# FFT long convolution and token mixer on one core: the first two second-stage chunks of the next group issued inside the inverse's first stage

## The chip, the cores and the metric

The kernel runs on one core of a Trainium2 chip. The metric is the device time of one execution in microseconds (us): 2053.82 us is the median of three runs (2049.52 to 2056.14).

The engines are named as the profile names them. PE is the matrix engine (TensorE) and PEld its weight loads, DVE is VectorE, ACT is ScalarE, POOL is GpSimd, and SP issues DMA transfers. PE can write only into PSUM, so each result has to be copied out by ACT or DVE; such a copy is called an eviction here.

## The reference

The first half is a long convolution along the sequence, done by FFT; the second is a token mixer.

```python
x, h: (8, 5696, 128), (5696, 128)
Xf = rfft(x, n=2 * S, axis=1); Hf = rfft(h, n=2 * S, axis=0)
x = irfft(Xf * Hf, n=2 * S, axis=1)[:, :S, :]
theta = x @ w_theta
zr, zi = x * cos(theta), x * sin(theta)
y = einsum('ts,bsd->btd', w_tok_r, zr) + einsum('ts,bsd->btd', w_tok_i, zi)
u = x + y
out = u + relu(u @ w_ch)          # w_tok_r, w_tok_i: (5696, 5696)
```

The change lies in the convolution alone, which fills less than the first fifth of the time. The mixer, whose two weight matrices are streamed in and transposed on the way, takes the rest.

## The kernel before, in words

**Groups.** The 8 batch rows and 128 channels are cut into 8 groups: two batch rows and 64 channels each. A transform of length 11392 is split as 178 x 64, and everything is done with matmuls against tables of sines and cosines. Each group goes through four stages:

- **A** (`stage_a`, matmuls L250): first stage of the forward transform, 16 chunks of 4 matmuls. The result is evicted by ACT (L259) into the tile `a`.
- **F** (`f2`, matmuls L270): second stage of the forward transform, 12 chunks F0 to F11. F0 to F10 have 32 matmuls each, F11 has 8, followed by 12 filler matmuls (L276). Each chunk is evicted by ACT into a tile `xs` (L426, called X here), of which there are two. DVE multiplies `xs` by the spectrum of the filter, `hs`, into `uv_t` (L428, and L433 for the last short chunk): this is the product P.
- **C** (`stage_c`, matmuls L448 and L449): first stage of the inverse, 16 chunks C0 to C15 of 16 matmuls. It reads `uv_t`. Each chunk is evicted into a column block of the tile `g`, by ACT (L453) or by DVE (L455).
- **D** (`stage_d`, matmuls L484): second stage of the inverse, 7 chunks D0 to D6. Each uses `g` over all its columns as weights, so D0 needs the evictions of all 16 C chunks. It is evicted into `yt`, by DVE (L488) for two chunks and by ACT (L490) for the others.

**The order.** The main loop (L772 to L798) has two halves per group g. In the first half, C of group g is mixed with A of group g + 1; I call it the CA half. In the second, D of group g is mixed with F, X and P of group g + 1; I call it the FD half. `woven` (L280) does the mixing: every list of steps gets a stretch of the interval 0 to 1, and the steps are issued in order of their positions. A goes to 0 to 0.88, C to 0.06 to 1.0, so that the tail of C has nothing beside it. There are seven passages from a CA half to an FD half in which both have work of the next group (g = 0 to 6); the eighth group has no successor.

Each engine runs its own instructions in the order of its queue. In the loop's steady state PE's order around the passage is A14 A15 C13 C14 C15 F0 F1 D0 F2 F3 D1 F4 D2 F5 F6 D3 F7 F8 D4 F9 F10 D5 F11 D6, and after it A0 A1 C0 of the next group's CA half.

**Who evicts.** In the CA half ACT takes all of A and the C chunks with `q % 32 == 16`, which are C2, C6, C10 and C14; DVE takes the 12 others. In the FD half ACT takes X0 to X11 and D1, D2, D4, D5 and D6; DVE takes P0 to P11, D0 and D3.

**Buffers.** All four stages draw their PSUM tiles from one pool of four (`fp`, L102), two banks each. There are two `xs` tiles (`fs`, L118) and four `hs` tiles (`fh`, L114). The product of chunk c issues the load of `hs` for chunk c + 4 on SP (L436). The loads of `x` for the group after next are issued by POOL (L153), each behind a small copy that reads an evicted column of `g` (L151).

Of the kernel before, what the change touches and what calls it, by code (L numbers as in the profile page):

```python
# [12 lines left out]
F16 = mybir.dt.float16  # L13
add = mybir.AluOpType.add
mult = mybir.AluOpType.mult
AF = mybir.ActivationFunctionType
# [6 lines left out]
def kernel(  # L23
# [10 lines left out]
    nc = tc.nc  # L34
    B, S, D = x.shape
    assert D == 128
    P = 128
# [42 lines left out]
    CK = 8  # L80
    HD = D // 2
# [5 lines left out]
    CHK = [(c0, min(CK, K1 - c0)) for c0 in range(0, K1, CK)]  # L87
    NCK = len(CHK)
    CN = 10
# [17 lines left out]
    LEAD = 4  # L107
# [11 lines left out]
    fs = pool("fft_s", 2, conv, side="right")  # L119
# [142 lines left out]
    def f2(a_st, c, warm=WARM):  # L262

        c0, ck = CHK[c]
        ps = psum()
        for j in range(ck):
            for ri in range(2):
                for e in range(2):
                    rows = slice(64 * e, 64 * e + 64)
                    nc.tensor.matmul(ps[:, e, j * HD:(j + 1) * HD],  # L270
                                     w_t2[rows, c0 + j, N2 * (1 - ri):N2 * (3 - ri)],
                                     a_st["a"][rows, ri * K1 + c0 + j, :],
                                     start=(ri == 0), stop=(ri == 1))
        if c == NCK - 1:
            for n in range(warm):
                nc.tensor.matmul(ps[:, n % 2, ck * HD:ck * HD + 384], w_t2[:, 2, :P],  # L276
                                 w_t2[:, 0:2, :].rearrange("p k n -> p (k n)"), start=True, stop=True)
        return ps[:, :, :ck * HD].rearrange("p e (k d) -> p e d k", k=ck)

    def woven(*lists):  # L280

        lists = [l if isinstance(l, tuple) else (l, 0.0, 1.0) for l in lists]
        steps = [(w0 + (i + 0.5) / len(l) * (w1 - w0), n, f)
                 for n, (l, w0, w1) in enumerate(lists) for i, f in enumerate(l)]
        for _, _, f in sorted(steps, key=lambda s: s[:2]):
            f()
# [37 lines left out]
    ps = psum()  # L324
# [82 lines left out]
    def stage_b(a_st, dh, warm=WARM, first=False):  # L407

        hs_of = {}

        def load(c):
            if c >= NCK:
                return
            hs = hs_of[c] = fh.tile([P, 2, HD * CK], F16, tag="hs", name="hs")
            if first:
                nc.sync.dma_start(hs[:64], hf_hbm[c, dh, :64])
                nc.sync.dma_start(hs[64:], hf_hbm[c, dh, :64, ::-1, :])
            else:
                nc.sync.dma_start(hs, hf_hbm[c, dh])

        def chunk(c):
            c0, ck = CHK[c]
            hv = hs_of[c].rearrange("p r (d k) -> p r d k", k=CK)
            ps = f2(a_st, c, warm)
            xs = fs.tile([P, 2, HD, CK], F16, tag="xs", name="xs")
            nc.scalar.activation(xs[:, :, :, :ck], ps, AF.Copy)  # L426
            if ck == CK:
                nc.vector.tensor_tensor(  # L428
                    uv[:, :, :, c0:c0 + ck],
                    xs.rearrange("p e d k -> p e (d k)").unsqueeze(1).to_broadcast([P, 2, 2, HD * CK]),  # L430
                    hv.rearrange("p r d k -> p r (d k)").unsqueeze(2).to_broadcast([P, 2, 2, HD * CK]), op=mult)
            for r in range(2 if ck < CK else 0):
                nc.vector.tensor_tensor(  # L433
                    uv[:, 2 * r:2 * r + 2, :, c0:c0 + ck], xs[:, :, :, :ck],
                    hv[:, r:r + 1, :, :ck].to_broadcast([P, 2, HD, ck]), op=mult)
            load(c + LEAD)  # L436
        return [lambda c=c: load(c) for c in range(LEAD)], [lambda c=c: chunk(c) for c in range(NCK)]

    def stage_c(st, last):

        def chunk(q):
            if q == 0:
                st["g"] = fg.tile([P, 2 * N2, P], F16, tag="g", name="g_")
            ps = psum()
            for i in range(8):
                o = ps[:, i // 4, (i % 4) * P:(i % 4 + 1) * P]
                at = (q + i) * K1
                nc.tensor.matmul(o, u_t[:, at:at + P], r_u, start=True, stop=False)  # L448
                nc.tensor.matmul(o[:, 2 * NP:], v_t[:, at:at + P], r_v, start=False, stop=True)  # L449
            g_out = st["g"][:K1, :, q:q + 8]  # L450
            g_in = ps[:K1].rearrange("p a (q c) -> p c (a q)", q=4)
            if (last and q % 16 == 0) or (not last and q % 32 == 16):
                nc.scalar.activation(g_out, g_in, AF.Copy)  # L453
            else:
                nc.vector.tensor_copy(g_out, g_in)  # L455
        return [lambda q=q: chunk(q) for q in range(0, 2 * HD, 8)]
# [16 lines left out]
    def stage_d(st, bp, dh, then=None):  # L473
        def chunk(n0, cn):
            if n0 == 0:
                st["yt"] = fy.tile([P, NB, N2], BF16, tag="yt", name="yt")
            g_, yt = st["g"], st["yt"]
            ps = psum()
            nq = 5 if cn == CN else cn
            for j in range(cn):  # L480
                o = ps[:, j // nq, (j % nq) * NB:(j % nq + 1) * NB]
                terms = terms_of(n0 + j)
                for i, (at, e_) in enumerate(terms):
                    nc.tensor.matmul(o, g_[:K1, at, :], e_, start=(i == 0), stop=(i == len(terms) - 1))  # L484
            y_out = yt[:, :, n0:n0 + cn].rearrange("p m (a q) -> p m a q", q=nq)
            y_in = ps[:, :cn // nq, :nq * NB].rearrange("p a (q m) -> p m a q", q=nq)
            if n0 in (0, 3 * CN):
                nc.vector.tensor_copy(y_out, y_in)  # L488
            else:
                nc.scalar.activation(y_out, y_in, AF.Copy)  # L490
            if n0 + cn == N2:
                if then is not None:
                    then(yt)
                for t0, t1 in [(H, S)] if then else YP:
                    for e in range(2):
                        with tc.issue_after(sides["row"]) if then else ExitStack():
                            (nc.gpsimd if then else nc.sync).dma_start(
                                yt_hbm[dh * HD:(dh + 1) * HD, 2 * bp + e, t0:t1],
                                yt[64 * e:64 * e + 64].rearrange("p m n -> p (m n)")[:, t0:t1])
        return [lambda n0=n0, cn=cn: chunk(n0, cn) for n0, cn in CHN]  # L500
# [4 lines left out]
    def front(g, by_dve=(), a_=None, spare=None):  # L505
        if g >= len(groups):
            return [], [], []
        bp, dh = groups[g]
        x16 = x16s[g].rearrange("p b n d -> p (b n) d")
        steps, a_st = stage_a(lambda q: x16[:NB, :, q], by_dve, a_, spare)  # L510
        return (steps, *stage_b(a_st, dh, WARM if g else WARM // 2, g == 0))

    a0, load0, b0 = front(0, (1, 3, 5, 8, 11, 13), a_0, (1, w_t2[:, 2:5].rearrange("p k n -> p (k n)"), 512 - 4 * K1))
# [258 lines left out]
    for g, (bp, dh) in enumerate(groups):  # L772
        st = {}
        last = g + 1 == len(groups)
        a_, load_, b_ = fronts.pop(g + 1) if g + 1 in fronts else front(g + 1)
        if last:
            for _ in range(3):
                steps0.pop(0)()
        now = ([with_load(steps0.pop(0), n < 6) for n in range(9)] if last else [], 0.0, 0.88)
        c_ = stage_c(st, last)  # L780
        if g == 0:
            ec = []
            swap_rows()
            now = ([lambda: ec.append(e_table(1)), lambda: ec.pop()(), lambda: ec.append(e_table(2)), lambda: ec.pop()(),
                    e_minus],
                   -0.1, 0.6)
        woven((c_, 0.06 if a_ else 0.0, 1.0), (a_, 0.0, 0.88), now, load_, (load_x(g + 2, st), 0.1, 1.02))
        if g == 0:
            ordered.close()
        if g + 2 == len(groups):  # L790
            xin.close()
            open_phases()
            load_ya0()
        now = [steps0.pop(0) for _ in range(5)] if last else []
        woven(b_, (stage_d(st, bp, dh, load_ya1 if last else None), 0.08 if b_ else 0.0, 1.1 if b_ else 1.0), now)
        if g + 2 == len(groups):
            load_ya1(st["yt"], True)
            open_ring()  # L798
# [305 lines left out]
    nxt, second, st = None, None, {}  # L1104
    ordered = ExitStack()
    for i, (k, p, tt, j0, s0, nj) in enumerate(stretches):
# [13 lines left out]
        if (p, tt, j0 + s0) == (0, 1, 0):  # L1120
            with tc.issue_after(sides["late"].ins):
# [4 lines left out]
        woven = (tt is not None and end_of_pair and i + 1 < len(stretches)  # L1126
                 and stretches[i + 1][2] is not None)
# [17 lines left out]
        if tt is None:  # L1145
            if p:
                aside(True, False)
            if first_of_pair:
                q = M1 if p else M3
# [20 lines left out]
            if end_of_pair:  # L1170
# [5 lines left out]
                c, c0 = c_last  # L1176
# [161 lines left out]
```

## Time and profile before

| quantity | value |
|---|---|
| median of three runs | 2053.82 us (2049.52 to 2056.14) |
| the profiled execution, its own time | 2052.18 us |
| its span, first to last instruction | 2050.4 us |
| PE busy | 1959.6 us, 96% of the span |
| DVE / ACT / POOL busy | 1538.9 / 639.9 / 965.2 us |
| mean granted clock of PE | 0.987 |
| FD halves of the 2nd to 7th passage start at | 129.8, 167.5, 205.7, 247.4, 285.9, 322.3 us |
| DVE eviction of one C chunk, L455 | 1219 ns |
| ACT eviction of one C chunk, L453 | 1021 ns |
| ACT eviction of one F chunk, L426 | 1023 ns |
| DVE / ACT eviction of one D chunk, L488 / L490 | 1080 / 917 ns |
| product of one chunk on DVE, L428 | 1224 ns |

The table is read like this. The span of the profiled execution is 1.8 us shorter than its own time, since something runs ahead of the first and behind the last instruction. PE is busy for nearly all of the span, so what counts is where PE stands still, and only that. The seven passages lie between 90 and 346 us; behind them only the last group's inverse belongs to the convolution. Their instructions are alike from the second passage on, so one of them, read closely, stands for the others. In the timeline a row of PE gives the start, the length, the line, the tiles, the count, and in brackets the idle time before it with what ended it.

### The profile page before, as it was taken

Reading aid. Unit: us, or ns where it says so; the run is one execution under the profiler, and the core shown is the slowest. Engines: PE = TensorE matmul, PEld = TensorE weight load, DVE = VectorE, ACT = ScalarE, POOL = GpSimd, SP = SyncE. Lnnn points to the kernel's source line nnn. Section 1 sums busy time; section 2 is a strip of 40 time slices with the busy share of each in tenths; the row PEclk is TensorE's granted clock in tenths of the full one; section 3 lists DMA queues with packets and bytes.
Section 4 is the critical chain, followed back from the end, with each engine's and each line's share of the span. In section 5 each row is a group of like instructions: output and inputs, shape, how many; then the busy total and the mean of one; then the engine's idle time right before and its main releaser. Section 6 shows DMA issues by size and latency. Waiting matters only on the chain.

```text
span 2050.4 us, 42565 instructions
## 1 busy us (share of the span) xinstructions
PE 1959.6 (96%) x16205; PEld 1086.2 (53%) x16381; DVE 1538.9 (75%) x2806; ACT 639.9 (31%) x936; POOL 965.2 (47%) x1769
## 2 busy tenths in 40 slices
PE   7799899799999999999999998999999999999998
PEld 5688888654444444444444443444444444444444
DVE  7787777657788888787867667867777686777767
ACT  6788777872232333333300000011111111111111
POOL 8323312384354545454566454453544535354450
PEclk9899999999999999999999999999999999999999
DMA  9999996999899998999999799797887969788793
GB/s 151 187 180 159 146 171 204 238 293 179 163 179 176 170 180 159 179 173 177 170 168 159 119 251 217 107 152 131 150 145 132 155 124 153 131 150 146 131 156 85
DMA packets 510158, 338.21 MB, mean 165 GB/s; under 512 B 184136, under 2 KB 461256, under 8 KB 509864
## 3 DMA queue, kind: packets, MB, share of 16 engines
q0 software_dynamic: 322368, 157.47, 61.0%
q1 hardware_dynamic: 181600, 166.48, 27.8%
q10 hardware_dynamic: 5984, 11.54, 1.6%
q8 instruction: 128, 2.10, 0.4%
q14 instruction: 78, 0.63, 0.1%
HBM read 379.54 MB, written 95.63 MB: 232 GB/s over the span
## 4 chain that ended last, share of the span: by engine, by line
PE 66%; DVE 3%; DMA 2%; issue 1%; POOL 0%; ACT 0%; DVEq 0%; ACTq 0%; SPq 0%
PE m L1275 62%; DMA b<-z_hbm 1%; DVE c L1282 1%; DVE b L831 1%; PE v L977 1%; PE utp L970 1%; PE m L1279 1%; DVE wt L890 1%; PE theta_ps L560 0%; PE tpz L918 0%; PE m L1162 0%; PE m L1196 0%; POOL ring L676 0%; DMA c<-cp_hbm 0%; DMA wl<-in_moe_w_tok_i_dram 0%
## 5 line engine op out<-in xcount | busy, mean ns | idle before, releaser
L676 POOL DMA_DIRECT2D ring<-in_moe_w_tok_i_dram x720 | 387.9, 546 | 657.7 <-DVE wt L890 576.9
L890 DVE STREAM_TRANSPOSE wt<-ring 128x384 f32<-128x384 f32 (+2 forms) x720 | 360.5, 527 | 127.7 <-PE m L1275 77.7
L676 POOL DMA_DIRECT2D ring<-in_moe_w_tok_r_dram x720 | 386.2, 547 | 142.4 <-DVE wt L890 82.4
L1275 PE MATMUL m<-b,wt 128*128 128x512 bf16 x1605 | 386.6, 380 | 3.7 <-DVE wt L890 1.7
L1275 PEld LDWEIGHTS <-wt 128*128 128x128 bf16 x1804 | 176.3, 98 | 219.5 <-DVE wt L890 7.4
L1282 DVE TENSOR_TENSOR c<-c,m 128x512 f32<-128x512 f32 x412 | 266.8, 674 | 0.4 <-PE m L1275 0.4
L972 ACT ACTIVATE ring<-utp 128x512 bf16<-128x512 bf16 x85 | 50.8, 597 | 582.1 <-PE utp L970 582.1
L428 DVE TENSOR_TENSOR uv_t<-xs,hs 128x2048 f16<-128x2048 f16 x88 | 104.4, 1224 | 29.9 <-ACT xs L426 18.2
L448 PE MATMUL ps<-r_u,uv_t 128*128 128x128 f16 x1024 | 116.5, 219 | 4.7 <-ACT cos L588 1.3
L1196 PE MATMUL m<-b,wt 128*128 128x512 bf16 x471 | 110.3, 379 | 7.6 <-DMA b<-z_hbm 4.2
L967 ACT ACTIVATE ub<-c 128x512 bf16<-128x512 f32 x88 | 55.1, 628 | 192.1 <-DVE c L1237 113.5
L449 PE MATMUL ps<-r_v,uv_t 128*128 128x100 f16 x1024 | 114.1, 207 | 0.5
L153 POOL DMA_DIRECT2D x<-in_x_dram x128 | 97.9, 771 | 22.2 <-POOL x L151 14.9
L426 ACT ACTIVATE xs<-ps 128x1024 f16<-128x1024 f32 x96 | 90.8, 972 | 42.4 <-PE ps L270 21.9
L449 PEld LDWEIGHTS <-uv_t 128*128 128x128 f16 x1024 | 99.9, 98 | 7.1 <-issue 5.7
L448 PEld LDWEIGHTS <-uv_t 128*128 128x128 f16 x1024 | 100.0, 98 | 1.1 <-DVE uv_t L433 0.4
L1196 PEld LDWEIGHTS <-wt 128*128 128x128 bf16 x528 | 50.4, 98 | 65.1 <-issue 8.4
L562 ACT ACTIVATE red<-theta_ps,magic 128x512 f32<-128x512 f32 (+1 forms) x46 | 31.6, 687 | 153.1 <-PE theta_ps L560 80.4
L270 PEld LDWEIGHTS <-w_t 64*128 64x128 f16 x3240 | 59.4, 100 | 32.1 <-issue 23.3
L920 ACT ACTIVATE ring<-tpz 128x512 bf16<-128x512 bf16 (+1 forms) x46 | 27.5, 597 | 132.6 <-PE tpz L918 116.3
L250 PE MATMUL ps<-f_t,x 89*128 89x180 f16 x512 | 62.8, 252 | 2.1 <-DVE a L257 1.1
L831 DVE TENSOR_TENSOR b<-b 128x1024 bf16<-128x1024 bf16 x100 | 61.4, 685 | 0.0
(2924 smaller groups left out, 3746.7 us busy)
## 6 DMA issues: line engine op xcount, KB each, us to landing
ring<-in_moe_w_tok_r_dram POOLq DMA_DIRECT2D x352, 96.0 KB, 4.6
ring<-in_moe_w_tok_i_dram POOLq DMA_DIRECT2D x352, 96.0 KB, 4.9
ring<-in_moe_w_tok_r_dram POOLq DMA_DIRECT2D x352, 80.0 KB, 4.5
ring<-in_moe_w_tok_i_dram POOLq DMA_DIRECT2D x352, 80.0 KB, 4.0
cp_hbm<-c SPq DMA_DIRECT2D x88, 256.0 KB, 2.6
c<-cp_hbm SPq DMA_DIRECT2D x88, 256.0 KB, 4.5
out_dram<-c SPq DMA_DIRECT2D x88, 256.0 KB, 4.5
hs<-hf_hbm SPq DMA_DIRECT2D x84, 256.0 KB, 3.4
```

The costliest lines, as they stand in the source:

```text
L153: nc.gpsimd.dma_start(x16[p0:p1, e, n0:n0 + 16, :HD], bass.AP(tensor=src.tensor, offset=src.offset + (p0 * N2 + n0) * D + dh * HD, ap=[[N2 ...
L250: nc.tensor.matmul(ps[:, i // 2, (i % 2) * 2 * K1:(i % 2 + 1) * 2 * K1], lhs(q + i), f1_t[:NB], start=True, stop=True)
L426: nc.scalar.activation(xs[:, :, :, :ck], ps, AF.Copy)
L428: nc.vector.tensor_tensor(uv[:, :, :, c0:c0 + ck], xs.rearrange("p e d k -> p e (d k)").unsqueeze(1).to_broadcast([P, 2, 2, HD * CK]), hv. ...
L448: nc.tensor.matmul(o, u_t[:, at:at + P], r_u, start=True, stop=False)
L449: nc.tensor.matmul(o[:, 2 * NP:], v_t[:, at:at + P], r_v, start=False, stop=True)
L676: nc.gpsimd.dma_start(wb[32 * i:32 * i + 32, :ng, :nj * 64], bass.AP(tensor=a.tensor, offset=a.offset + row0 * S + p * H + i * QR + j0 * 6 ...
L831: return [lambda f=f, x=x: f(*x) for f, x in ((nc.vector.tensor_sub, (bt[M3], b12, b22)), (nc.vector.tensor_sub, (bt[M4], b21, b11)), (nc. ...
L890: nc.vector.transpose(wt.rearrange("p j t r -> p (j t r)").bitcast(F32).rearrange("p (j g t) -> p g j t", j=TJ, g=4)[:, :ng, :nj], wb[:, : ...
L1196: nc.tensor.matmul(ms[n // 2 * 2 + h], a[n][:, j, :, r], bts_of[p][jj][n % 2 * 2 + h][:, r, :], start=(n % 2 == 0 and jj == 0 and r == 0), ...
L1275: nc.tensor.matmul(ms[q], a[q][:, j, :, r], bts[jj][q][:, r, :], start=(jj == 0 and r == 0), stop=(jj == NJ - 1 and r == 1 and q not in left))
L1282: nc.vector.tensor_tensor(c, z, ms[q], op=op)
```

## The change

It has four edits, all in the convolution.

1. `chunk` of the forward second stage is cut into `spectrum` (the matmuls F and the eviction X) and `products` (P and the next load of `hs`). For every group but the first, the spectra of chunks 0 and 1 become the first two steps of the list, and their products the next two.
2. In the main loop the first two steps of that list are taken out of the FD half and woven into the CA half, at 0.84 to 1.0. The products stay behind, at the head of the FD half. A's stretch is shortened from 0.88 to 0.82.
3. Of the C chunks ACT now takes those with `q % 48 == 32`, which are C4 and C10. DVE takes the 14 others, among them C11 to C15.
4. D0 is evicted by ACT, no longer by DVE, except in the last group.

```diff
+        def spectrum(c):
+            ps = f2(a_st, c, warm)
+            xs = xs_of[c] = fs.tile([P, 2, HD, CK], F16, tag="xs", name="xs")
+            nc.scalar.activation(xs[:, :, :, :CHK[c][1]], ps, AF.Copy)
+
+        def products(c):
             c0, ck = CHK[c]
             hv = hs_of[c].rearrange("p r (d k) -> p r d k", k=CK)
-            ps = f2(a_st, c, warm)
-            xs = fs.tile([P, 2, HD, CK], F16, tag="xs", name="xs")
-            nc.scalar.activation(xs[:, :, :, :ck], ps, AF.Copy)
+            xs = xs_of.pop(c)
...
-        return [lambda c=c: load(c) for c in range(LEAD)], [lambda c=c: chunk(c) for c in range(NCK)]
+        def chunk(c):
+            spectrum(c)
+            products(c)
+
+        ahead = 2 if a_st["ahead"] else 0
+        return ([lambda c=c: load(c) for c in range(LEAD)],
+                [lambda c=c: spectrum(c) for c in range(ahead)] + [lambda c=c: products(c) for c in range(ahead)] +
+                [lambda c=c: chunk(c) for c in range(ahead, NCK)])
...
-            if (last and q % 16 == 0) or (not last and q % 32 == 16):
+            if (last and q % 16 == 0) or (not last and q % 48 == 32):
...
-            if n0 in (0, 3 * CN):
+            if n0 in ((0, 3 * CN) if then else (3 * CN,)):
...
+        a_st["ahead"] = g > 0
...
-        woven((c_, 0.06 if a_ else 0.0, 1.0), (a_, 0.0, 0.88), now, load_, (load_x(g + 2, st), 0.1, 1.02))
+        first, b_ = b_[:2], b_[2:]
+        woven((c_, 0.06 if a_ else 0.0, 1.0), (a_, 0.0, 0.82), (first, 0.84, 1.0), now, load_, (load_x(g + 2, st), 0.1, 1.02))
```

## The prediction

> **What bounds the kernel now.** I read the busy shares first, then the waits of the convolution, then one passage in the timeline, engine by engine.
>
> ```profile
> PE 1959.6 (96%) x16205; PEld 1086.2 (53%) x16381; DVE 1538.9 (75%) x2806; ACT 639.9 (31%) x936; POOL 965.2 (47%) x1769
> ```
>
> PE is busy 96% of the span. The change moves PE work without adding or removing any (the built program has the same 32764 PE rows, matmuls and weight loads, in another order), so only PE's idle time can change. The waits between 67 and 366 us show whether a delay there reaches the end:
>
> ```profile
> POOL ring L676 <- PE ps L276: 16.5, 1, 16.5
> ```
>
> The mixer's weight stream starts only when the last filler matmuls of F are through, so what the convolution loses or gains shifts the mixer too. I count it in full.
>
> Next, PE and DVE around the passage at 130 us:
>
> ```profile
> 129.63 0.21 PE L449 MATMUL ps<-r_v,uv_t 128*128 128x100 f16 x1
> 129.77 1.11 PE L270 MATMUL ps<-a__2458,w_t 64*128 64x64 f16 x64
> 131.25 1.21 PE L484 MATMUL ps<-e_t,g__2471 90*128 90x89 f16 x26 [0.36 <-DVE g__2471 L455]
> ```
>
> ```profile
> 128.28 1.22 DVE L455 CAST g__2471<-ps 90x1024 f16<-90x1024 f32 x1 [0.23 <-PE ps L449]
> 129.88 1.22 DVE L455 CAST g__2471<-ps 90x1024 f16<-90x1024 f32 x1 [0.38 <-PE ps L449]
> 131.51 2.36 DVE L428 TENSOR_TENSOR uv_t<-xs,hs 128x2048 f16<-128x2048 f16 x2 [0.41 <-ACT xs L426]
> ```
>
> C15 leaves PE at 129.77. Its eviction runs on DVE from 129.88 to 131.10, and D0, which needs all of `g`, starts 0.15 us later. F0 and F1 lie in that gap and fill 1.11 us of 1.48. What stays is 0.36 us of idle PE, the same in passages 2 to 7 (0.47 in the first). **F0 and F1 are thus the cover of the last eviction**, and they are what the change moves ahead.
>
> Then the rest of the FD half:
>
> ```profile
> 141.22 0.47 PE L270 MATMUL ps<-a__2458,w_t 64*128 64x64 f16 x20 [0.95 <-issue]
> ...
> 145.49 0.84 PE L484 MATMUL ps<-e_t,g__2471 90*128 90x89 f16 x16 [0.73 <-issue]
> ```
>
> ```profile
> 298.39 0.47 PE L270 MATMUL ps<-a__6710,w_t 64*128 64x64 f16 x20 [0.51 <-DVE yt L488]
> ```
>
> In passages 2 to 7 PE waits for an evicting engine (by over 0.12 us, as far as a gap is listed) only at D0 and this once: F9 waits 0.51 us for the buffer of D3, in passage 6. All other idle time there is "issue": 0.95 + 0.73 in passage 2; 0.81 + 1.21 + 0.19 in 3; 0.21 + 3.33 in 4; 0.22 + 2.70 in 5; 0.16 in 6; 2.13 + 0.45 in 7; with 0.37 in the first, 13.5 us in all. Counted in the program, these gaps sit 256 PE instructions apart or a multiple of that, and where two follow at once their ends are 4.27 us apart (141.22 and 145.49; 175.92, 180.19 and 184.47). The page has 128 transfers of the kind "instruction" with 2.10 MB, 16 KB each. So I read them as PE waiting for the next block of its program, asked for when the block before is entered.
>
> **The change, part by part.**
>
> *F0 and F1 move ahead.* In the built order PE runs A14 A15 C12 C13 F0 C14 F1 C15 D0 F2 F3, where it ran A14 A15 C13 C14 C15 F0 F1 D0 F2 F3; from D0 on nothing differs. PE reaches the end of C15 1.11 us later than it did, with the same work done, and D0 follows with nothing between. Its wait is then 0.11 (C15 leaving PE to DVE) + 1.22 (the eviction) + 0.15 (DVE to PE) = 1.48 us in place of 0.36: **+1.12 us**. X0 and X1 leave PE sooner, which nothing on PE waits for. F0 needs A15's eviction: with ACT at 0.66 us from one A to the next behind C10 and A13, it ends some 0.1 us ahead of F0. If that cover fails, F0 waits a few tenths.
>
> *C evictions: 14 on DVE, 2 on ACT.* The CA half is PE's (19.2 us busy of 19.3 in the windows from 266.6 on), with DVE at 13.7 and ACT at 15.9 us. DVE gets 2 x 1.22 more, 16.1; ACT loses 2 x 1.02 and gets X0 and X1, 2 x 1.02: no change. Both stay under PE. The order matters more: C11 to C15 now all go to DVE, at 1.17 us each. With C10's end at 0 on PE, C11 to C15 leave PE at 1.14, 2.62, 3.42, 4.75 and 6.08 (0.80 a C chunk, 0.34 an A, 0.53 an F). DVE ends C12 at 3.9 and C13 at 5.1, and starts C14 and C15 within 0.1 us of PE: nothing, up to 0.08. I take **1.15 us a passage**; the bounds are 1.05 (a gap shorter by what the modelled ends of matmuls hide) and 1.30.
>
> *D0 to ACT; less work in the FD half.* DVE loses 1.08 of 16.1 us there; ACT loses 2 x 1.02 and gets 0.92, 14.4 to 13.3. Neither is what PE waits for. F9's wait for D3 stays, since D3 is still behind P0 to P6 on DVE: 0 in my sum, between -0.5 and +0.2 in one passage. X2 now stands behind D0's eviction on ACT, P2 behind X2, C0 behind P11: X2 comes at D0 + 2.2 (1.15 of D0, 0.1, 0.92), against F2's end at D0 + 1.7. DVE, whose P0 and P1 are then done, absorbs this, and PE has four buffers ahead. If not, 0.5 us a passage. In the first passage D1 and D2 stand ahead of X2 on ACT in either program; I count 1.15 there too.
>
> *Loads.* SP's order and POOL's are the same. The loads of `hs` hang on P, the last loads of `x` on C12 and C14; measured from D0, both move by under 0.5 us. I count nothing; what it can cost is an "issue" gap more or less.
>
> *Waiting for program blocks.* PE's extra wait gives a block time to arrive if it was asked for ahead of the wait and used behind it. By the count of instructions that is so in passages 4 and 5, whose first gaps are 0.21 and 0.22: **-0.4 us**. In the others the block in question is entered behind D0's start.
>
> **Sum:** 7 x 1.15 - 0.4 = +7.6 us. From the profiled execution's own 2052.18 that gives 2059.8; the median of the runs is 1.6 higher, which gives 2061.4. I say **2061**, +0.37%.
>
> **The rivals.**
>
> *The wait is hidden behind the program blocks.* If a block's arrival, rather than PE, sets the pace from before D0 on, PE waits longer at D0 and less at the next "issue" gaps. For it: the gaps are there in every passage, 4.27 us apart. Against it: the asking hangs on PE's own position. Each passage gives back at most 1.15 and what its gaps hold: 5 x 1.15 + 0.37 + 0.16 = 6.3. That leaves +1.8: 2056, no measurable change.
>
> *Half the clock.* Two stretches ran at half clock, seen in the windows of 2 us:
>
> ```profile
> 218.00:220.00 2.00, 2.00 (x30) 2.00 (x27) 1.07 (x1) 0.90 (x1) 0.00 (x0) 0.50 0.34 128
> ...
> 334.00:336.00 2.00, 1.71 (x23) 1.43 (x22) 2.00 (x3) 0.64 (x1) 0.00 (x0) 0.50 0.66 216
> ```
>
> The column behind the bracketed counts is PE's granted clock. They begin at 216.3 and 332.3, behind the gaps of 3.33 and 2.13 us, and last 6.8 and 10.2 us, costing some 3 and 5. The gap of 2.70 in passage 5 brought none. A gap of 1.5 us between matmuls as sparse as D's could bring more: one gives 2065, three 2073. The Trainium skill ("TensorE: Matmul & The Clock Gate", "The HAM clock gate") says that the clock falls after an idle window of about 3.4 us; by that a gap of 1.5 us costs nothing beyond itself, and the sum stays. The trace agrees at 3.33 and not at 2.13, so the rival keeps a chance.
>
> *Faster, by program blocks that come in time.* F uses instructions fastest (32 matmuls in 0.53 us). With 128 of them drawn out of the FD half and a longer wait at its head, the fetch might gain enough lead that the "issue" gaps and with them the half-clock stretches go: at most 13.5 + 8 = 21.5 us, so 2061.4 + 0.4 - 21.5 = 2040. It turns the sign once it saves 8 us, and is measurable from 14.3 on. Against it: the 256-instruction blocks behind D0 hold what they held.
>
> That the change doesn't do what it says is excluded by the built order.
>
> **How the numbers follow.** 0.3% of 2053.8 is 6.2 us, about what a measurement of this kernel can tell from no change; above 2060.0 is "slower". Chances: my forecast 0.56, with its own range of 2057 to 2065 (bounds of the passage, and runs that scatter by 3 us); hidden 0.20; half clock 0.17; faster 0.07. Of my forecast some 0.40 lies above 2060.0. Slower: 0.40 + 0.17 = 0.57. Same: 0.16 + 0.20 + 0.01 = 0.37. Faster: 0.06. The range is 2055 to 2069; it leaves out the faster case, the low end of the hidden one and more than one or two added half-clock stretches.
>
> **What would show it.** In the timeline D0's bracket should read about 1.5 us behind DVE's eviction of `g` in all seven passages; the FD half behind D0 should be as long as before, but for "issue" gaps; DVE's products P0 and P1 should start at C15's eviction end without a wait. I am wrong if D0's bracket stays under 0.8, if the "issue" gaps fall well under 13 us in sum, or if PE waits for `xs`, `yt` or `uv_t` where it did not.

## The result

The changed kernel takes 2056.22 us (median of 19 runs, 2052.49 to 2063.69), the kernel before 2049.52 us (median of 19 runs, 2044.3 to 2056.14). The ratio is 1.0035, 95% interval 1.0025 to 1.0045: slower by 7.2 us, between 5.1 and 9.2. The kernel before came out 4.3 us lower over 19 runs than over the three that the prediction had, so 2061 stood for +7.6 us, of which 7.2 were measured. The same kernel run again beside other runs of the kernel before gave 1.0020, 1.0009 to 1.0031, or +4.1 us. The two intervals overlap from 1.0025 to 1.0031.

The page of the changed kernel, first the busy shares (compare 1959.6, 1538.9 and 639.9 before):

```profile
PE 1965.8 (96%) x16205; PEld 1088.5 (53%) x16381; DVE 1546.8 (75%) x2813; ACT 632.1 (31%) x929; POOL 967.4 (47%) x1769
```

The same 16205 PE records are busy for 6.2 us more. This sum alone shows little, because the execution also ran 67 us at half clock, against 52 us in the profile before, which alone is worth up to 7 us; what part belongs to the change is read from the windows below. Next the wait that ties the mixer to the convolution, from the waits between 67 and 372 us:

```profile
POOL ring L689 <- PE ps L276: 17.6, 1, 17.6
```

The mixer still starts behind the last filler matmuls. From their end to the end of the span it is 1704.4 us before and 1704.3 us after, and 1704 to 1708 us in all the kernels below: what happens in the convolution reaches the end.

The passage that the prediction read, now on PE and on DVE:

```profile
130.83 0.64 PE L270 MATMUL ps<-a__2458,w_t 64*128 64x64 f16 x32
...
132.31 0.64 PE L270 MATMUL ps<-a__2458,w_t 64*128 64x64 f16 x32
...
135.18 1.23 PE L496 MATMUL ps<-e_t,g__2471 90*128 90x89 f16 x26 [1.32 <-DVE g__2471 L467]
```

```profile
130.14 3.50 DVE L467 CAST g__2471<-ps 90x1024 f16<-90x1024 f32 x3 [0.36 <-PE ps L461]
133.90 1.22 DVE L467 CAST g__2471<-ps 90x1024 f16<-90x1024 f32 x1 [0.26 <-PE ps L461]
135.04 2.35 DVE L433 TENSOR_TENSOR uv_t<-xs,hs 128x2048 f16<-128x2048 f16 x2
```

F0 and F1 stand alone among the C chunks, and D0 waits 1.32 us for the eviction that ends at 135.12. The brackets of the other passages read 1.36, 1.31, 1.32, 1.31, 1.32 and 1.31, where they read 0.36 (0.47 in the first). P0 follows the eviction without a wait, as foretold.

The rest of that FD half has the same kind of gaps as before, and none of another kind. Over all seven FD halves the "issue" gaps sum to 11.9 us, against 13.5 before. In this one:

```profile
141.78 0.96 PE L270 MATMUL ps<-a__2458,w_t 64*128 64x64 f16 x53 [0.84 <-issue]
...
145.51 0.46 PE L270 MATMUL ps<-a__2458,w_t 64*128 64x64 f16 x19 [0.65 <-issue]
...
150.33 0.79 PE L496 MATMUL ps<-e_t,g__2471 90*128 90x89 f16 x15 [1.25 <-issue]
```

The windows view shows what the brackets don't. The windows run from D6 to D0 (the CA half) and from D0 to about the next D6 (the FD half) in the second and fourth passage; the columns are length, then busy time and count of PE, PEld, DVE, ACT and POOL, PE's clock, and DMA. Before:

```profile
110.73:131.25 20.52, 20.08 (x395) 19.60 (x393) 15.40 (x15) 17.06 (x24) 9.71 (x19) 1.00 1.21 170
131.25:148.44 17.19, 15.32 (x484) 13.45 (x485) 14.84 (x13) 13.60 (x15) 3.59 (x6) 1.00 0.98 178
186.64:207.18 20.54, 20.09 (x394) 19.58 (x393) 14.93 (x14) 17.03 (x23) 9.75 (x19) 1.00 1.25 157
207.18:228.35 21.17, 17.63 (x484) 15.72 (x485) 15.03 (x13) 13.31 (x15) 3.56 (x6) 0.84 0.79 138
```

After:

```profile
113.10:135.18 22.08, 20.65 (x394) 19.66 (x392) 17.21 (x17) 16.35 (x22) 10.20 (x19) 1.00 1.15 153
135.18:153.20 18.02, 15.28 (x484) 13.42 (x485) 13.87 (x12) 12.93 (x14) 3.19 (x6) 1.00 0.89 171
192.00:214.14 22.14, 20.71 (x394) 19.66 (x393) 17.21 (x17) 16.35 (x22) 10.20 (x19) 1.00 1.28 153
214.14:229.70 15.56, 14.91 (x484) 13.32 (x485) 13.79 (x12) 13.03 (x14) 3.22 (x6) 1.00 0.87 173
```

The CA half is longer by about 1.56 us, not by the 0.96 of the bracket, and 0.57 to 0.62 of it is PE "busy" for the same matmuls. The FD half varies far more, by issue gaps and by the clock (0.84 in one window before, 1.00 in the three others).

### The profile page after: what moved, and what is told of

It reads as the page before. It is cut to its first block, busy times and chain, and to the rows that moved or that the text cites. A ratio compares the mean times of both kernels' runs of the same rounds, so it can differ in the third digit from the quotient of the medians.

```text
span 2056.2 us, 42557 instructions
## 1 busy us (share of the span) xinstructions
PE 1965.8 (96%) x16205; PEld 1088.5 (53%) x16381; DVE 1546.8 (75%) x2813; ACT 632.1 (31%) x929; POOL 967.4 (47%) x1769
## 4 chain that ended last, share of the span: by engine, by line
PE 65%; DMA 3%; DVE 3%; issue 1%; POOL 1%; ACT 0%; DVEq 0%; ACTq 0%
PE m L1289 61%; DMA b<-z_hbm 2%; DVE c L1296 1%; PE v L991 1%; PE utp L984 1%; PE m L1293 1%; DVE b L845 1%; POOL ring L689 1%; PE theta_ps L573 0%; DVE wt L904 0%; PE tpz L932 0%; PE m L1176 0%; DMA ring<-in_moe_w_tok_i_dram 0%; PE m L1210 0%; DMA wl<-in_moe_w_tok_i_dram 0%
```

## The experiments

All 11 kernels and the repeat are told here. Lengths are taken from one profile each: the CA half from the end of the last filler row to D0's start, mean of passages 2 to 7, which agree within 0.06 us in every kernel. "Rest" is the CA half less D0's bracket. "Sum of seven" adds up how much longer the seven CA halves are than in the kernel before, the first (22.18 us before) included. A bracket of 0.07 is read from the rows' times; the timeline lists no gap so short.

| kernel | CA half | bracket | rest | first CA half | sum of seven | measured ratio (95%) | in us |
|---|---|---|---|---|---|---|---|
| before | 20.36 | 0.36 | 20.00 | 22.18 | | | |
| changed | 21.91 | 1.32 | 20.60 | 24.53 | +11.7 | 1.0035 (1.0025 to 1.0045) | +7.2 |
| changed, again | 21.92 | 1.32 | 20.60 | 24.05 | +11.3 | 1.0020 (1.0009 to 1.0031) | +4.1 |
| e1 sharing alone | 20.94 | 0.94 | 20.00 | 23.34 | +4.7 | 1.0019 (1.0005 to 1.0034) | +3.9 |
| e2 moves alone | 22.02 | 1.40 | 20.61 | 24.14 | +11.9 | 1.0049 (1.0034 to 1.0064) | +10.0 |
| e3 one F behind C15 | 21.55 | 1.06 | 20.49 | 23.68 | +8.7 | 1.0056 (1.0040 to 1.0073) | +11.5 |
| e5 C15 split, changed | 22.59 | 1.98 | 20.61 | 25.03 | +16.2 | 1.0087 (1.0069 to 1.0105) | +17.8 |
| e6 C15 split, before | 20.47 | 0.48 | 20.00 | 22.78 | +1.3 | 1.0003 (0.9988 to 1.0017) | +0.6 |
| e7 C15 on ACT, before | 20.20 | 0.07 | 20.13 | 22.56 | -0.6 | 0.9991 (0.9976 to 1.0007) | -1.8 |
| e9 D0 on ACT alone | 20.37 | 0.36 | 20.01 | 22.16 | +0.1 | 0.9999 (0.9986 to 1.0012) | -0.2 |
| e10 A in 0.82 alone | 20.66 | 0.36 | 20.29 | 23.21 | +2.8 | 1.0006 (0.9992 to 1.0019) | +1.2 |
| e11 A in 0.88, changed | 22.11 | 1.31 | 20.80 | 24.26 | +12.6 | 1.0047 (1.0030 to 1.0065) | +9.6 |
| e12 C15 and D0 on ACT, before | 20.20 | 0.07 | 20.13 | 22.85 | -0.2 | 0.9998 (0.9987 to 1.0009) | -0.4 |

e4 moves F2 and F3 ahead of D0, so its halves don't compare; it is told below. The theory under test: what the change costs is the last C eviction, which no longer has F0 and F1 beside it. The rivals: the new sharing of evictions, the half clock, the program blocks.

**e1: edits 3 and 4 alone.**

```diff
 (kernel before)
-            if (last and q % 16 == 0) or (not last and q % 32 == 16):
+            if (last and q % 16 == 0) or (not last and q % 48 == 32):
...
-            if n0 in (0, 3 * CN):
+            if n0 in ((0, 3 * CN) if then else (3 * CN,)):
```

> Edits 3 and 4 alone (C evictions 14 on DVE and 2 on ACT, D0 on ACT), PE's order as before. Uncovered last eviction: C13, C14 and C15 leave PE 0.8 us apart and all queue on DVE at 1.17 us each, so C15's eviction ends some 0.75 us later behind C15 than before; D0's bracket goes from 0.36 to about 1.0, 7 x 0.65 = +4.5 us, ratio 1.002. Rival (the new sharing is free or a relief, DVE and ACT being off PE's path): bracket 0.36, ratio 1.000 or under. Rival (the program blocks set the pace): bracket about 1.0 but the issue gaps smaller by as much, ratio 1.000.

PE and DVE in the same passage:

```profile
131.36 1.11 PE L270 MATMUL ps<-a__2458,w_t 64*128 64x64 f16 x64
133.41 1.23 PE L484 MATMUL ps<-e_t,g__2471 90*128 90x89 f16 x26 [0.94 <-DVE g__2471 L455]
```

```profile
129.87 3.48 DVE L455 CAST g__2471<-ps 90x1024 f16<-90x1024 f32 x3 [0.24 <-PE ps L449]
```

The three evictions at the end of the CA half now queue behind one another on DVE, and D0 waits 0.94 us with F0 and F1 still in front of it. Measured 1.0019, expected 1.002. The sharing is no relief; it is a second way to make the last eviction late.

**e2: edits 1 and 2 alone.** The changed kernel with the old conditions of e1's diff.

> Edits 1 and 2 alone (F0 and F1 ahead of C14 and C15), the evictions shared as before. Uncovered last eviction: D0's bracket 1.25 to 1.32 in each of the seven passages, as in the changed kernel, +6.5 us on the kernel before, ratio 1.003. Rival (the cost is the new sharing): bracket as in the changed kernel or less, ratio under 1.001. Rival (half clock): ratio depends on stretches at 0.50, not on the bracket.

The bracket is 1.40 to 1.51 in all seven passages and the ratio 1.0049. So the move costs as much without the new sharing as with it: in the changed order C14's eviction is done before C15 leaves PE, whoever does it. Here ACT does, and DVE's eviction of C15 runs from 134.00 to 135.22:

```profile
132.54 1.01 ACT L465 ACTIVATE g__2471<-ps 90x1024 f16<-90x1024 f32 x1
```

```profile
135.37 0.81 PE L496 MATMUL ps<-e_t,g__2471 90*128 90x89 f16 x16 [1.41 <-DVE g__2471 L467]
```

**e4: other F chunks as cover.**

```diff
 (changed kernel)
-        woven(b_, (stage_d(...), 0.08 if b_ else 0.0, 1.1 if b_ else 1.0), now)
+        woven(b_, (stage_d(...), 0.26 if b_ else 0.0, 1.1 if b_ else 1.0), now)
```

> The changed kernel with D set back in the FD half (its stretch begins at 0.26, not 0.08), so that PE runs C15 F2 F3 D0 F4 D1: two other F chunks stand where F0 and F1 stood. Uncovered last eviction: D0's bracket falls from 1.32 to about 0.3, -7 us on the changed kernel, back to the kernel before, ratio 0.999 to 1.001. Rival (the loss is in the order or the sharing as such, whatever stands ahead of D0): ratio stays at 1.003. X2 waits for P0, which waits for C15's eviction; if that holds a PSUM buffer too long, PE waits at D1 or F5, up to 0.5 us a passage.

The ratio is 1.0059 (1.0041 to 1.0078), +12.1 us: a miss. PE in the same passage, then ACT and DVE:

```profile
134.62 1.23 PE L496 MATMUL ps<-e_t,g__2471 90*128 90x89 f16 x26 [0.28 <-DVE g__2471 L467]
...
136.86 1.38 PE L496 MATMUL ps<-e_t,g__2471 90*128 90x89 f16 x30 [0.44 <-ACT xs L426]
...
139.71 1.37 PE L496 MATMUL ps<-e_t,g__2471 90*128 90x89 f16 x30 [0.26 <-ACT xs L426]
...
147.17 0.64 PE L270 MATMUL ps<-a__2458,w_t 64*128 64x64 f16 x32 [0.85 <-DVE yt L500]
```

```profile
135.79 2.16 ACT L426 ACTIVATE xs<-ps 128x1024 f16<-128x1024 f32 x2 [2.28 <-DVE uv_t L433]
```

```profile
133.34 1.22 DVE L467 CAST g__2471<-ps 90x1024 f16<-90x1024 f32 x1 [0.26 <-PE ps L461]
134.48 4.72 DVE L433 TENSOR_TENSOR uv_t<-xs,hs 128x2048 f16<-128x2048 f16 x4
```

D0's bracket falls to 0.28 as expected, and the wait comes back further on. X0 and X1 hold both `xs` tiles until P0 and P1, and these stand behind C15's eviction on DVE. ACT waits 2.28 us for P0, F2 and F3 keep their PSUM buffers meanwhile, and PE waits for them at D1 and D2, then for D3's eviction: 1.0 to 2.2 us of such waits in each of passages 2 to 6. The condition that I had written down as costing "up to 0.5 us a passage" cost three times that. These waits are not the whole account of the 12.1 us: in this profile the "issue" gaps sum to 4.5 us only, and 31 us of the FD halves ran at half clock, against 13.5 and 17 us in the kernel before. A third `xs` tile would tell whether the cover pays without it; it was not tried.

**e3: one F behind C15.** The changed kernel with `first` woven at (0.90, 1.06): PE runs C13 C14 F0 C15 F1 D0.

> The changed kernel with F0 and F1 each one C chunk later: PE runs C13 C14 F0 C15 F1 D0, so that F1 alone covers the last eviction. Uncovered last eviction: C14 and C15 queue on DVE, the bracket is about 0.95 (1.32 less 0.53 of F1, plus 0.2 that C15 waits on DVE), 7 x 0.6 = +4 us on the kernel before, ratio 1.002, between the kernel before and the changed one. Rival (drawing F out of the FD half is the loss): ratio as for the changed kernel, 1.0035.

The bracket is 1.06 (0.95 expected). The ratio, 1.0056, is far above the 1.002 that I gave and not below the changed kernel's. The table shows a part of why: the rest is 20.49, not 20.00. Its CA halves sum to +8.7 us, inside the interval of 8.2 to 15.0 us. Why it isn't cheaper than the changed kernel, whose CA halves are longer, wasn't shown; 27 us of the FD halves of its one profile ran at half clock.

**e5: the last eviction cut in two.**

```diff
 (changed kernel)
+            if not last and q == 2 * HD - 8:
+                for a in range(2):
+                    half = st["g"][:K1, :, q + 4 * a:q + 4 * a + 4], ps[:K1, a].rearrange("p (q c) -> p c q", q=4)
+                    if a == 0:
+                        nc.scalar.activation(*half, AF.Copy)
+                    else:
+                        nc.vector.tensor_copy(*half)
+            elif ...
```

> The changed kernel, with C15's eviction cut in two halves of 512 columns, one on ACT and one on DVE. Uncovered last eviction: its length falls from 1.22 to about 0.7 us, D0's bracket from 1.32 to about 0.8, -3.5 us on the changed kernel, ratio to the kernel before 1.0015 to 1.002. Rival (the bracket is not the eviction's length but something else ahead of D0, a program block or the A15 wait): bracket stays at 1.3, ratio 1.003.

The bracket went the other way, to 1.98, and the ratio to 1.0087. ACT, DVE and PE show why:

```profile
133.97 0.58 ACT L468 ACTIVATE g__2472<-ps 90x512 f16<-90x512 f32 x1
```

```profile
133.96 1.23 DVE L433 TENSOR_TENSOR uv_t<-xs,hs 128x2048 f16<-128x2048 f16 x1 [0.32 <-PE ps L461]
135.10 0.68 DVE L470 CAST g__2472<-ps 90x512 f16<-90x512 f32 x1
```

```profile
135.85 0.82 PE L503 MATMUL ps<-e_t,g__2472 90*128 90x89 f16 x16 [1.98 <-DVE g__2472 L470]
```

The halves are as short as expected (0.58 and 0.68 us), but in the built program DVE runs P0 ahead of its half, which then ends at 135.78. D0 starts 0.07 us later. The edit became the opposite of what was meant, and it serves the theory as a dose: 0.66 us more of bracket a passage, and the dearest kernel of all.

**e6, e7, e9: the kernel before, varied.** e6 cuts C15's eviction as in e5; e7 gives ACT `q % 32 == 24`, so C15 and not C14; e9 is edit 4 alone.

> The kernel before, with C15's eviction cut in two halves of 512 columns, ACT's and DVE's, and nothing else. Uncovered last eviction: it ends at about C15 + 0.95 instead of + 1.48 us, under the 1.11 of F0 and F1, so D0's bracket of 0.36 goes: -2.5 us, ratio 0.9988. Rival (the bracket of the kernel before costs nothing, since issue gaps behind it give it back): ratio 1.000.

> The kernel before, with ACT taking C3, C7, C11 and C15 instead of C2, C6, C10 and C14: the last eviction costs 1.02 instead of 1.22 us. Uncovered last eviction: bracket 0.36 to about 0.15, -1.5 us, ratio 0.9993, within the noise. Rival as for the split kernel: 1.000.

> Edit 4 alone: D0 evicted by ACT, all else as before. Uncovered last eviction: D0's bracket is unchanged at 0.36, X2 stands behind D0's eviction with nothing on PE waiting for it: ratio 1.000. Rival (the share of evictions in the FD half counts): a relief of DVE would give 0.999, a delay of X2 1.001 with new brackets that name xs.

e6: the bracket didn't go, it rose to 0.48, and the ratio is 1.0003. DVE starts its half only when ACT has finished its own, so the two halves run one behind the other, 0.58 and 0.69 us:

```profile
129.69 0.58 ACT L456 ACTIVATE g__2472<-ps 90x512 f16<-90x512 f32 x1
```

```profile
130.30 0.69 DVE L458 CAST g__2472<-ps 90x512 f16<-90x512 f32 x1 [1.12 <-ACT g__2472 L456]
```

The edit cut the eviction, but it didn't shorten it. e7: the bracket went (0.07 is left), but PE then waits at F4 for D0's buffer:

```profile
134.43 0.64 PE L270 MATMUL ps<-a__2458,w_t 64*128 64x64 f16 x32 [0.71 <-DVE yt L488]
```

and its ratio of 0.9991 is not clear of 1. e9 is 0.9999: who evicts D0 is indifferent, as the prediction had it.

**e10 and e11: the rest of the CA half.** The 0.60 us by which the rest grew needed a cause. e10 is the kernel before with A woven at 0 to 0.82; e11 is the changed kernel with A back at 0 to 0.88.

> The kernel before with A's stretch shortened to 0.82 and nothing else. From the last C filler to D0, less D0's bracket, the kernel before takes 20.0 us a passage and the changed one 20.6, at the same work. If the second pair of A chunks that the 0.82 brings is part of that, this kernel takes 20.2 to 20.3, bracket 0.36, ratio 1.0007; if the 0.6 comes from F among the C chunks alone, it takes 20.0, ratio 1.000.

> The changed kernel with A's stretch back at 0.88: PE runs A14 A15 C13 F0 C14 F1 C15 D0. F among the C chunks costs about 0.3 us a passage at the turns from C to F and back (0.90 for a C chunk ahead of F against 0.80, 0.58 for F against 0.52), so 20.3 without the bracket if nothing else; but F0 now stands one C chunk (0.8 us) behind A15, whose eviction takes about 1.3, so F0 waits up to 0.5 us. Bracket 1.3. Ratio 1.004 to 1.006. If F0 doesn't wait, 1.003.

The CA half of the third passage, before and in e10:

```profile
148.44:168.96 20.52, 20.08 (x395) 19.58 (x392) 14.92 (x14) 17.03 (x23) 9.73 (x19) 1.00 1.32 154
```

```profile
150.02:170.83 20.81, 20.35 (x395) 19.60 (x392) 14.98 (x14) 16.81 (x23) 9.51 (x19) 1.00 1.27 148
```

It is 0.29 us longer at an unchanged bracket of 0.36, nearly all of it PE "busy" (20.35 against 20.08): half of the 0.60. In e11 a wait appears that the changed kernel doesn't have, at F0:

```profile
169.43 0.64 PE L270 MATMUL ps<-a__3521,w_t 64*128 64x64 f16 x32 [0.40 <-ACT a__3521 L259]
```

Its rest is 20.80. Less that 0.40 it is 20.40, of which 0.40 over the kernel before is what is left for F among the C chunks. So the shorter stretch for A is paid with 0.3 us and saves 0.4.

**e12: both last evictions on ACT.** e7 and e9 together, on the kernel before.

> The kernel before with C15 and D0 both evicted by ACT (C3, C7, C11, C15 on ACT; D0 on ACT). C15 on ACT alone took D0's bracket away and brought a wait of 0.52 to 0.71 at F4 for D0's buffer, whose eviction stood behind P0 and P1 on DVE. With D0 on ACT that wait goes too: 7 x 0.36 = -2.5 us on the kernel before, ratio 0.9988. Rival (issue gaps give it back, or X2 behind D0 on ACT makes a new wait): 1.000.

PE in the passage:

```profile
130.43 1.11 PE L270 MATMUL ps<-a__2458,w_t 64*128 64x64 f16 x64
131.61 1.23 PE L484 MATMUL ps<-e_t,g__2471 90*128 90x89 f16 x26
132.77 1.11 PE L270 MATMUL ps<-a__2458,w_t 64*128 64x64 f16 x64
```

D0 has no bracket any more, and the wait at F4 is gone. But 0.07 us of it stays unlisted and the rest grew by 0.13, so that 0.16 us a passage is left, and the first passage loses 0.67. The ratio is 0.9998 (0.9987 to 1.0009). No version here beats the kernel before by what these runs can tell.

**The changed kernel again.**

> The changed kernel once more, for a second profile and a ratio of its own. From the last C filler to D0 its passages are 1.56 us longer than in the kernel before (0.96 of D0's bracket, 0.30 of the second pair of A chunks, 0.30 of the turns between C and F) and the first 2.35: 11.7 us, against 7.2 measured. If that sum is the whole, the ratio here is 1.0057. If the FD half gives some back (issue gaps under the 13.5 us of the kernel before), it is 1.0035 again, and the issue gaps of this profile sum to 9 to 12 us.

1.0020, below both values that I gave. The CA halves of passages 2 to 7 repeat to 0.02 us, the issue gaps sum to 9.7 us. The whole sum of 11.3 is therefore not what the kernel pays; the FD half or the clock gives some of it back.

## Why the prediction was right, and where not

**The uncovered eviction: right, a little too large.** Taken as +1.15 us a passage, it measured +0.96 (1.32 against 0.36). The kernel before has 0.15 us between the end of the last eviction and D0, and I carried that over; in the changed kernel it is 0.06 (135.12 to 135.18). e2, with the old sharing, has 0.15 again (135.22 to 135.37) and a bracket of 1.40. So the new sharing, which I had priced at nothing, gives about 0.09 us back; by what path, wasn't shown. The other 0.1 us isn't saved: the bracket counts from the modelled end of the last matmul, which lies further behind a C matmul than behind an F matmul, and this 0.1 stands in the rest. e1 and e5 move the bracket without the move of F (0.94) and beyond it (1.98), and the measured times follow.

**"From D0 on nothing differs", "the same work done": the step that was incomplete.** I priced the new order in the CA half at the durations of its matmuls and let only waits cost something. The CA half also grew by 0.60 us that no bracket names: 0.29 by the second pair of A chunks (shown by e10), and the other 0.3 to 0.4 where F stands among C chunks. The rows show about 0.2 of the latter: there is one more C chunk with an F behind it, which takes 0.90 us where others take 0.80, and each lone F takes 0.57 where two take 1.04. A further 0.1 is the part of the wait that the bracket leaves out.

**The first passage: wrong.** Counted at 1.15, its CA half grew by 2.35 (1.87 in the repeat). The bracket makes 0.89 of it. PE is "busy" for 0.61 us more in the repeat, as in the other passages, and for 1.30 us more in the first profile. That passage also has waits of its own, which I hadn't worked out, but they explain little: ahead of D0 they sum to 1.73 us before, 1.87 in the changed kernel and 2.22 in the repeat. In the profile of the changed kernel this half also ran at a granted clock of 0.95, against 1.00 before and 0.99 in the repeat; 0.05 of 24.5 us is up to 1.2 us of matmul time.

**What comes back: the block term was right where it was placed, and too small as a sum.** I allowed 0.4 us in passages 4 and 5. Their first gaps of 0.21 and 0.22 are gone. But the CA halves sum to +11.7 and +11.3, and the kernel is slower by 7.2 and 4.1. So 4 to 7 us come back, not 0.4. That a forecast of 7.6 met 7.2 is in part two misses that cancel.

**Where it comes back is seen in the profiles; why stays open.** The seven FD halves are shorter in both profiles of the changed kernel than in the one before. Three things account for the difference, by sums over the seven halves:

| us | before | changed | changed, again |
|---|---|---|---|
| length of the FD halves | 132.2 | 127.4 | 123.1 |
| "issue" gaps | 13.5 | 11.9 | 9.7 |
| listed waits for an evicting engine behind D0, most of them in the first passage | 3.4 | 1.9 | 2.5 |
| time at half clock, of which half is lost | 17.1 | 13.7 | 6.8 |
| left without the gaps, the waits and half of the last | 106.9 | 106.8 | 107.5 |

But the profiles of the six kernels that don't move F (e1, e6, e7, e9, e10, e12) spread as widely: 125 to 132 us of FD halves, with 9.7 to 12.7 us of "issue" gaps and 6.8 to 17.1 us at half clock. So single profiles don't show that the change brought this about, and the prediction's own sign of being wrong, "issue" gaps well under 13 us, decides nothing either.

One thing shows over many runs: the mean granted clock of the changed kernel is 0.9866 over its 19 runs and 0.9877 over the 12 of the repeat, against 0.9845 in the 17 runs of the kernel before beside that repeat (0.9843 to 0.9852 beside the experiments). If the throttled stretches are all at half clock, as those in the traces are, that is 55 and 51 us against 64 us, or 4.3 and 6.5 us of matmul time. It is of the right size: 4.5 and 7.2 us come back. But the same reckoning fails for e10 (0.9873 against 0.9851), where it would give 4.5 us back and the difference between +2.8 and +1.2 is 1.6. Which stretches they are, and why fewer, wasn't shown.

**The rivals.** "Half clock" falls: over the runs there was less of it, not more, so gaps of 1.3 us between C and D brought none on balance. (In one point the prediction read the trace loosely: the half clock that it puts behind the 3.33 us gap began at 216.2 us, when that gap, from 213.80 to 217.13, had lasted 2.4 us.) "Hidden behind the program blocks" had a true core, since a good part came back, though not all of it. But smaller "issue" gaps are only a part of that (1.6 and 3.8 us in the two profiles), and kernels that don't move F have gaps as small. "Faster" asked that the fetch of the program gain enough lead for these gaps, and the half clock behind them, to go, by 8 us at least; 11.9 and 9.7 us of gaps are still there, and the kernel is slower in both sets of runs.

## What to carry to other kernels

Work that stands between a producer's last step and its first consumer is cover; before moving it ahead, add up producer to evicting engine, eviction, evicting engine to consumer, and see what is left to stand there. Replacing the cover by later work of the same chain only helps if that work's own buffers are free by then (e4). And a timeline's idle brackets are no full account of PE: compare the length of one stage, from one fixed row to another, before and after.

## What the runs showed of the hardware that was not expected

- A stall can hide in "busy". Two A chunks in a row take 0.65 us at the end of the CA half in the kernel before, and 0.79 and 0.85 us in the changed one, where a single one takes 0.34. The next C matmul there starts 0.22 and 0.28 us behind the last A matmul's start, otherwise 0.08; the timeline puts no bracket there, since it gives that A matmul a modelled length of 0.24 us or so. What PE waits for wasn't shown.
- Where matmuls of 128 rows (C) are followed by matmuls of 64 rows (F), about 0.1 us more goes by: a C chunk with an F behind it takes 0.90 us against 0.80, and a lone F of 32 matmuls 0.57 against 0.52 in a pair.
- The "issue" gaps belong to places in the program. Counted over PE's rows in the trace, matmuls and weight loads, every listed "issue" gap behind D0 lies 193 to 195 rows past a multiple of 256, in all 14 profiles; this bears out the reading as waits for blocks of 256 instructions. Where one such wait follows the other at once, they end 4.27 us apart: 185.64 and 189.91 us in the changed kernel, 175.92, 180.19 and 184.47 us in the kernel before.
- Two engines that each evict half of one PSUM tile into one tile of SBUF ran one behind the other in e6: DVE's half started 0.03 us behind the end of ACT's. Whether the chip or the order of the program asks for that wasn't shown.
